# Strided attention of batch 3 in two visits of quarter-array matmuls instead of six of full-array ones, with a second buffer for the transposed strided keys

## The chip, the core and the metric

The kernel runs on one core of a Trainium2 chip. A core has a matmul engine (PE, here called by its matmuls; PEld are its weight loads, which overlap them), a vector engine (DVE), a scalar engine (ACT), a general engine (POOL) and a queue engine (SP). Each works through its own list of instructions in order, and they wait for one another by semaphores. PE writes only to PSUM, eight banks of 2 KiB per partition; DVE and ACT read it from there. Transfers between the memory outside of the core and SBUF are issued here by POOL (with a cast from f32 to bf16) and by SP (transposes and outputs), and run on 16 DMA engines.

The metric is the time of one execution on the device in microseconds, lower is better. Times of single instructions come from a profiled execution.

## The reference

Attention with two kinds of heads, then a two-layer network with a squared ReLU:

```python
B, H, S, D = 8, 8, 576, 64; stride = 32
scores = q @ k.T / sqrt(D)
mask_local = (rel >= 0) & (rel < stride)                  # heads 0 to 3, rel = row - column
mask_strided = (rel >= 0) & (column % stride == row % stride)   # heads 4 to 7
attn = softmax(where(mask, scores, -1e9))
x = (attn @ v).transpose(0, 2, 1, 3).reshape(4608, 512)
out = (relu(x @ w_in) ** 2) @ w_out                       # 512 -> 2048 -> 512
```

In a strided head a token attends to the earlier tokens of its own residue modulo 32, 18 at most. So such a head splits into 32 separate problems of 18 by 18.

## The kernel before

**Main loop.** After batch 0, which has a list of its own, the program is one list of 288 groups of matmuls: nine chunks c of 512 tokens, each with 16 groups of the first layer (`mm1`, L863) and 16 of the second (`mm2`, L969). A group is four matmuls of 512 columns, except in the last two chunks. Chunk 2 is groups 64 to 95 and chunk 3 groups 96 to 127; chunk 3 (tokens 1536 to 2047) is the first that reads attention of batch 3 (tokens 1728 to 2303). A first-layer group goes to one of two PSUM banks (4 and 5), from which ACT takes the ReLU (L869) and DVE the square (L873). A second-layer bank is copied by ACT to `y` (L973), every fourth group, and sent out on SP's queue (L977).

**Attention between the groups.** The text `PLAN` names for each group the attention steps that are put into the program ahead of it. A step issues its matmuls there, and may put off what follows on ACT and DVE by some groups (`later`, `tick`; `put_off` does it for bank readers). The order on every engine is thus the order of this text; nothing is rearranged afterwards. Steps of the local heads are `G` (scores of a batch's two pairs, L599, then the exponentials L610 and masks L606), `D` (outputs, L822, with L827 and L828) and `E` (DMA transpose into `xt`, L837). `xt` are the four tiles of transposed attention that `mm1` reads.

**Banks of the attention steps.** After group 32 they have six banks (6, 7, 0, 1, 3 and 2) in a list, and each use moves a bank to the list's end. `bank("pt")` takes the first; `bank_two` takes the pair of neighbours that was used longest ago. `step_G` takes all six, in order, and fills them two at a time:

```python
bk = [bank("pt") for _ in range(6)]
bk = [bk[0::2], bk[1::2]]
...
nc.tensor.matmul(bk[row][t // 4][:, c:c + QL], ...)
```

**Strided heads, two ways.** The four strided heads of a batch are packed so that three heads of one residue make a block of 54 by 54 (the fourth head's residues are packed by three). `OLD` names the batches that use the first way.

- *Full array* (batches 1 and 3): two residues of odd and even parity lie on the diagonal of one 128 by 128 weight tile whose rest is zero. Keys are copied into `kbd` (`step_K`, L382 and L386, one visit for each parity), values into `vbd` (`spread_v_str`, L447). Scores take three visits (`s3.0`, `s3.1`, `s3.2`: `step_SS`, L623, exponential L624, mask L626), outputs three (`x3.0` to `x3.2`: `step_XX`, sums L634, outputs L637, logarithm L640, exponential L642, products L650 and L657).
- *Quarter array* (batches 2, 4, 5, 6, 7): matmuls with 64 by 64 weights, four at a time on the four quarters. Scores take one visit (`s4`: `step_S4`, L687 straight from the transposed keys, L692 from the copy `kcs` of the fourth head), in four banks; outputs one visit (`x4+2+5`: `step_X4`, sums L751, outputs L756), in three pairs of banks for parts 0, 1 and 2. ACT takes logarithm and exponential of the sums of a part (L722, L723), DVE multiplies (six L735 for part 0, six for part 1, four L728 for part 2). The two numbers say by how many groups the work of parts 1 and 2 on ACT and DVE is put off.

**Loading.** POOL loads strided keys and queries in rows (`k_t`, `q_t`, L365), SP transposes them by DMA into `kT_s` and `qT_s` (L370; steps `Xnk`, `Xnq`). There are two buffers for `qT_s` and one for `kT_s`. Values come by POOL: two loads into `v_st` for the first way (L440, L443), four into `v_s` for the second (L432, L436).

In the plan, batch 3 stands like this: keys copied ahead of groups 68 and 69, scores at 72, 73 and 76, outputs at 75, 88 and 90. `G4`, the score step of batch 4's local heads, stands ahead of group 94.

Of the kernel before, what the change touches and what calls it, by code (L numbers as in the profile page):

```python
# [67 lines left out]
56: C4k C4q  # L68
57: V3 R12kv
58: V4 R12qa  # L70
60: B30v
61: B31v R13qv
62: R13ka
63: U4
64: X4q
66: Y17
67: Y16 C5q
68: k30v
69: k31v
70: X4k  # L80
71: C5k Q20k Q21q Q20q
72: Q21k s3.0
73: s3.1
75: x3.0
76: s3.2
80: G3
81: H3v
84: D12.0 D13.0
85: D12.1 D13.1
86: E12  # L90
87: E13
88: x3.1
90: x3.2
93: H4v
94: G4
96: k41v
# [53 lines left out]
def kernel(  # L150
# [24 lines left out]
    NP2 = STRIDE // 2  # L175
    NG = 5
    NH = NG + 1
    OLD = (1, 3)
    NB = NP2 + NH
    NS = NP2 // 2  # L180
    W3 = 3 * NA
# [9 lines left out]
    rows = ctx.enter_context(ExitStack())  # L191
# [7 lines left out]
    v_st = rows.enter_context(tc.tile_pool(name="v_st", bufs=1, side="right"))  # L199

    PS = bass.MemoryType.PSUM
    strTs = {nm: rows.enter_context(tc.tile_pool(name=f"strT{nm}", bufs=n, side="right")) for nm, n in (("q", 2), ("k", 1))}
    psum = ctx.enter_context(tc.tile_pool(name="psum", bufs=1, space=PS))
    psb = psum.tile([128, 8, 512], FP32, name="psb")
    all_banks = [psb[:, i] for i in range(8)]
# [171 lines left out]
    def step_K(b, par, copy):  # L377
        o = str_T[b, "k"]
        r = slice(64 * par, 64 * par + 64) if b in OLD else slice(0, 128)
        kb = kbd[r, :, 64 * par:64 * par + W3]  # L380
        if b in OLD:
            copy(kb[:, 0:NP2], o[r, 0:NP2, 0:W3])  # L382
        to = kb[:, NP2:NB] if b in OLD else kcs[b % 2][:, :, 0:W3]
        src = o[r, :, W3:SP_]
# [42 lines left out]
    def load_v_str(b):  # L427
        if b not in OLD:
            t = vs_pool.tile([128, (2 * NS + NH) * D], BF16, name="v_s")
            w, wh = 2 * NS * D, NH * D  # L430
            for f in range(2):
                nc.gpsimd.dma_start(out=t[64 * f:64 * f + W3, 0:w],  # L432
                                    in_=v[b, 4:7].rearrange("h (m r) d -> (h m) (r d)", r=STRIDE)[:, w * f:w * (f + 1)])
                src = v[b, 7]
                src = bass.AP(src.tensor, src.offset + wh * f, [[2 * NG * D, 3], [RW, NA], [1, wh]])
                nc.gpsimd.dma_start(out=t[64 * f:64 * f + W3, w:w + wh], in_=src)  # L436
            v_str[b] = t
            return
        t = v_st.tile([W3, 2 * NB * D], BF16, name="v_st")
        nc.gpsimd.dma_start(out=t[:, 0:RW], in_=v[b, 4:7].rearrange("h (m r) d -> (h m) (r d)", r=STRIDE))  # L440
        src = v[b, 7]
        src = bass.AP(src.tensor, src.offset, [[2 * NG * D, 3], [RW, NA], [1, 2 * (NG + 1) * D]])
        nc.gpsimd.dma_start(out=t[:, RW:2 * NB * D], in_=src)  # L443
        v_str[b] = t
# [727 lines left out]
    for line in PLAN.strip().splitlines():  # L1172
        n, words = line.split(":")
# [42 lines left out]
```

## Time and profile before

| what | us |
|---|---|
| median of 3 runs (lowest to highest) | 296.67 (295.76 to 296.91) |
| the profiled execution | 296.19 |
| its span, first to last instruction | 294.5 |
| PE busy | 285.5 |
| DVE busy | 206.3 |
| ACT busy | 169.4 |
| POOL busy | 85.5 |

The two kinds of matmuls of the main loop, L863 with 130.8 us and L969 with 99.2 us, hold most of PE's time. Their mean duration of 379 ns is longer than their distance, since one begins while the one before it drains; where a row gives a length, the distance to the start of the next row is what a piece of work costs.

How to read a row of the timeline: start and length in us, engine, line, operation, output and inputs, tile or shape, count, and in brackets how long the engine stood still before it and what ended that. A row with a count is several equal instructions put together. A few matmul records can be missing, so a count may be one short. In the list of waits the columns are who waited, for whom, total, times and longest.

### The profile page before, as it was taken

What the parts mean: (1) busy time and instruction counts of PE and PEld (TensorE: products, weight loads), DVE (VectorE), ACT (ScalarE), POOL (GpSimd) and SP (SyncE); (2) the same over time, 40 slices, a digit from 0 to 9 for tenths busy, and PEclk for the clock granted to TensorE, in tenths of its full rate; (3) what the DMA queues carried; (4) which work ended last, traced back from release to release, by engine and by line L of the source; (5) the groups of instructions that cost most, each with busy time, mean ns of one, the idle gap of its engine ahead of it and who ended that gap; (6) DMA issues with size and microseconds to landing.
All of it is one profiled execution on the core that took longest, in us unless ns stands there. A gap on an engine that the chain in (4) does not pass through costs nothing.

```text
span 294.5 us, 6425 instructions
## 1 busy us (share of the span) xinstructions
PE 285.5 (97%) x2441; PEld 153.6 (52%) x2477; DVE 206.3 (70%) x531; ACT 169.4 (58%) x320; POOL 85.5 (29%) x133
## 2 busy tenths in 40 slices
PE   7899999999999999999999999999999999999994
PEld 3554555544445454454445444454444444984594
DVE  5667797685577755667367836683389979958983
ACT  3767846774758736674567446654675566206610
POOL 8884443073025036146400940000000014103300
PEclk9999999999999999999999999999999999999999
DMA  7999999999999999989997997521011210030003
GB/s 144 187 210 208 198 202 183 212 212 101 135 249 140 153 168 173 184 107 138 216 158 132 136 217 138 108 58 73 36 20 48 82 38 1 0 115 30 1 2 142
DMA packets 91086, 37.23 MB, mean 126 GB/s; under 512 B 77392, under 2 KB 83896, under 8 KB 91056
## 3 DMA queue, kind: packets, MB, share of 16 engines
q0 software_dynamic: 49968, 18.14, 58.9%
q1 hardware_dynamic: 40944, 18.62, 31.6%
q8 instruction: 19, 0.31, 0.4%
q14 instruction: 11, 0.09, 0.1%
q10 hardware_dynamic: 144, 0.07, 0.1%
HBM read 36.83 MB, written 9.44 MB: 157 GB/s over the span
## 4 chain that ended last, share of the span: by engine, by line
PE 93%; DMA 3%; issue 1%; POOL 1%; DVE 0%; DVEq 0%; POOLq 0%
PE psb L863 42%; PE psb L969 33%; PE psb L939 9%; DMA vl<-in_v_dram 3%; PE psb L822 2%; PE psb L599 1%; PE psb L502 1%; PE psb L554 1%; PE psb L751 1%; PE psb L687 1%; PE psb L756 1%; POOL xt L306 0%; PE psb L637 0%; PE psb L844 0%; PE psb L623 0%
## 5 line engine op out<-in xcount | busy, mean ns | idle before, releaser
L863 PE MATMUL psb<-xt,w_in 128*128 128x512 bf16 x557 | 130.8, 379 | 0.9
L869 ACT ACTIVATE r<-psb 128x512 bf16<-128x512 f32 x144 | 85.6, 599 | 46.2 <-PE psb L863 43.0
L969 PE MATMUL psb<-w_out_b,g_sb 128*128 128x512 bf16 x432 | 99.2, 379 | 1.4 <-issue 0.8
L863 PEld LDWEIGHTS <-w_in 128*128 128x128 bf16 x576 | 53.7, 98 | 60.0 <-issue 1.1
L873 DVE TENSOR_TENSOR g_sb<-r 128x512 bf16<-128x512 bf16 x112 | 46.8, 422 | 39.9 <-ACT r L869 38.7
L969 PEld LDWEIGHTS <-g_sb 128*128 128x128 bf16 x448 | 41.8, 98 | 47.5
L973 ACT COPY y<-psb 128x512 f32<-128x512 f32 x28 | 16.6, 591 | 38.9 <-PE psb L969 38.8
L908 POOL CAST sa<-g_sb 128x256 fp32r<-128x256 bf16 x16 | 9.6, 603 | 96.6 <-DVE g_sb L903 96.6
L735 DVE TENSOR_TENSOR xt<-psb,rv 64x144 bf16<-64x144 f32 x60 | 18.7, 311 | 9.2 <-ACT rv L723 8.4
L828 DVE TENSOR_TENSOR x_l<-psb,rinv 96x384 bf16<-96x384 f32 x28 | 15.5, 553 | 1.0
L606 DVE TENSOR_TENSOR e<-e,mask_all 128x576 bf16<-128x576 bf16 x20 | 8.4, 458 | 10.5 <-ACT e L610 10.3
L903 DVE TENSOR_TENSOR g_sb<-r 128x512 bf16<-128x512 bf16 x32 | 13.0, 420 | 2.9 <-ACT r L869 2.9
L610 ACT ACTIVATE e<-psb 128x384 bf16<-128x384 f32 x30 | 12.0, 513 | 4.2 <-PE psb L599 4.2
L365 POOL DMA_DIRECT2D q_t<-in_q_dram x6 | 3.2, 536 | 38.1 <-DMA qT_s<-q_t 22.4
L294 POOL DMA_DIRECT2D k_l<-in_k_dram x16 | 11.7, 736 | 4.1 <-DMA k_t<-in_k_dram 1.6
L294 POOL DMA_DIRECT2D q_l<-in_q_dram x16 | 11.6, 732 | 3.4 <-DMA k_t<-in_k_dram 2.0
L939 PE MATMUL psb<-t,s 128*128 128x256 f32 x96 | 12.2, 283 | 0.0
L365 POOL DMA_DIRECT2D k_t<-in_k_dram x6 | 3.3, 553 | 30.2 <-DMA kT_s<-k_t 28.2
L939 PEld LDWEIGHTS psb<-t,s 128*128 128x128 f32 x96 | 11.6, 188 | 0.0
L951 DVE TENSOR_TENSOR y<-psb,y 128x256 f32<-128x256 f32 x19 | 8.1, 424 | 4.3 <-PE psb L939 3.5
L453 POOL DMA_DIRECT2D vl<-in_v_dram x8 | 9.8, 1227 | 3.7 <-PE psb L969 2.8
L650 DVE TENSOR_TENSOR xt<-psb,rv 64x144 bf16<-64x144 f32 x24 | 7.5, 311 | 4.5 <-ACT rv L642 4.2
(153 smaller groups left out, 321.8 us busy)
## 6 DMA issues: line engine op xcount, KB each, us to landing
out_dram<-y SPq DMA_DIRECT2D x35, 256.0 KB, 2.8
vl<-in_v_dram POOLq DMA_DIRECT2D x8, 288.0 KB, 9.1
w_out_b<-in_moe_w_out_dram POOLq DMA_DIRECT2D x4, 512.0 KB, 14.9
q_t<-in_q_dram POOLq DMA_DIRECT2D x7, 288.0 KB, 6.6
k_t<-in_k_dram POOLq DMA_DIRECT2D x7, 288.0 KB, 6.3
w_in<-in_moe_w_in_dram POOLq DMA_DIRECT2D x2, 768.0 KB, 13.5
k_l<-in_k_dram POOLq DMA_DIRECT2D x16, 72.0 KB, 8.1
q_l<-in_q_dram POOLq DMA_DIRECT2D x16, 72.0 KB, 7.2
```

The source lines that it names most:

```text
L294: nc.gpsimd.dma_start(out=t[:, :, hh, :], in_=src[b, 2 * p + hh].rearrange("(t p) d -> p t d", p=QL))
L453: nc.gpsimd.dma_start(out=t[32:128, :, :, :, 0:D].rearrange("p u h t d -> p (u h t) d"), in_=v[b, 0:4].rearrange("h (t p) d -> p (h t) d", ...
L610: nc.scalar.activation(e[:, row, 4 * QL * i:4 * QL * (i + 1)], bk[row][i][:, 0:4 * QL], AF.Exp, scale=scale)
L735: nc.vector.tensor_tensor(to[:, :, :, n * part:n * (part + 1), par], both[half(par), :, 0:w].rearrange("c f (a h m) -> c h m f a", a=n, h= ...
L828: nc.vector.tensor_tensor(x, po[0:QL, :, 0:D], rinv[0:QL].to_broadcast([QL, NL, D]), op=ALU.mult)
L863: nc.tensor.matmul(ph, w_in_tile(kk, ff), xt[kk][:, 512 * c:512 * (c + 1)], start=(kk == order[0]), stop=(kk == order[-1]))
L869: nc.scalar.activation(r, ph, AF.Relu)
L873: later(1, lambda: nc.vector.tensor_tensor(g[:, ff, :], r, r, op=ALU.mult))
L903: nc.vector.tensor_tensor(g[:, ff, :], r, r, op=ALU.mult)
L939: nc.tensor.matmul(pa, a, b, start=k == 0 and n not in "273", stop=k == 7, skip_group_check=True)
L969: nc.tensor.matmul(py, g[:, ff, 128 * j:128 * (j + 1)], w_out_b[:, ff, :], start=(ff == 0), stop=(ff == 15))
L973: nc.scalar.copy(y, py)
```

## The change

`3` is taken out of `OLD`, so that batch 3 goes the second way; the plan's steps for it become one score visit at group 72 and one output visit at group 88, with the work of part 1 put off by one group and that of part 2 by three. Its values are loaded by four transfers into `v_s`, at the same place in the list. The copies into `vbd` (`B30v`, `B31v`) and one of two key copies (`k30v`) go; `k31v` now copies the fourth head's keys into `kcs`. Transposed strided keys get a second buffer, so that a key transpose of any later batch does not wait for the score visit of the batch before it (`step_S4` reads them directly, and with one buffer batch 4's transpose, ahead of group 70, would stand ahead of batch 3's score visit at 72).

```diff
-60: B30v
-61: B31v R13qv
+61: R13qv
...
-68: k30v
 69: k31v
 70: X4k
 71: C5k Q20k Q21q Q20q
-72: Q21k s3.0
-73: s3.1
-75: x3.0
-76: s3.2
+72: Q21k s3
 80: G3
 81: H3v
-84: D12.0 D13.0
+83: D12.0 D13.0
 85: D12.1 D13.1
 86: E12
 87: E13
-88: x3.1
-90: x3.2
+88: x3+1+3
 93: H4v
 94: G4
...
-    OLD = (1, 3)
+    OLD = (1,)
...
-    strTs = {nm: rows.enter_context(tc.tile_pool(name=f"strT{nm}", bufs=n, side="right")) for nm, n in (("q", 2), ("k", 1))}
+    strTs = {nm: rows.enter_context(tc.tile_pool(name=f"strT{nm}", bufs=n, side="right")) for nm, n in (("q", 2), ("k", 2))}
```

The outputs `D12.0` and `D13.0` of the local heads move one group forward. On PE the six visits (44 score matmuls, 6 of sums and 44 of outputs in batches 1 and 3 together, so 22, 3 and 22 here) are replaced by 44 score matmuls, 12 of sums and 44 of outputs on quarters of the array. SP's list keeps the same instructions in the same order; POOL's has two loads more.

## The prediction

> **What bounds the kernel now.** I read the page first (engines, slices, chain), then the waits of the matmul engine, then its timeline around the two places that change.
>
> ```profile
> span 294.5 us, 6425 instructions
> PE 285.5 (97%) x2441; PEld 153.6 (52%) x2477; DVE 206.3 (70%) x531; ACT 169.4 (58%) x320; POOL 85.5 (29%) x133
> PEclk9999999999999999999999999999999999999999
> PE 93%; DMA 3%; issue 1%; POOL 1%; DVE 0%; DVEq 0%; POOLq 0%
> ```
>
> PE is busy 97% of the span and is 93% of the chain that ended last. DVE at 70% and ACT at 58% hang on it. The clock row has a 9 in all 40 slices.
>
> ```profile
> PE psb L986 <- DVE xt L1101: 1.3, 1, 1.3
> PE psb L969 <- issue: 0.8, 5, 0.2
> PE psb L554 <- DVE kTl L509: 0.4, 1, 0.4
> ```
>
> These are the three longest waits of PE (total, times, longest). The first and third belong to batch 0. Behind them PE waits for no engine and no transfer, only five times for "issue", never over 0.2 us. So a change in the middle counts in full if it takes matmul time away from PE or makes PE wait, and counts nothing if it only relieves DVE, ACT or a queue.
>
> **The change, part by part.** First the matmuls themselves. This is PE's timeline from the first scores of batch 3 to the score step of the local heads of batch 4 (G4). The columns are start, length, line, names, shape and count. Lengths overlap since matmuls are pipelined, so I price a visit from its start to the start of what follows it.
>
> ```profile
> 90.37 0.36 PE L623 MATMUL psb<-qT_s,kb 128*128 128x54 bf16 x8
> 90.58 1.02 PE L863 MATMUL psb<-xt,w_in 128*128 128x512 bf16 x4
> 91.44 0.37 PE L623 MATMUL psb<-qT_s,kb 128*128 128x54 bf16 x8
> 91.64 1.89 PE L863 MATMUL psb<-xt,w_in 128*128 128x512 bf16 x8
> 93.37 0.35 PE L634 MATMUL psb<-e,ones_bd 128*128 128x432 bf16 x1
> ...
> 93.77 1.02 PE L863 MATMUL psb<-xt,w_in 128*128 128x512 bf16 x3
> 94.63 0.31 PE L623 MATMUL psb<-qT_s,kb 128*128 128x54 bf16 x6
> 94.78 3.69 PE L863 MATMUL psb<-xt,w_in 128*128 128x512 bf16 x16
> 98.40 0.69 PE L599 MATMUL psb<-qT,kTl 64*128 64x96 bf16 x24
> 99.02 3.63 PE L969 MATMUL psb<-w_out_b,g_sb 128*128 128x512 bf16 x15
> ...
> 106.67 0.35 PE L634 MATMUL psb<-e,ones_bd 128*128 128x432 bf16 x1
> ...
> 107.07 1.89 PE L969 MATMUL psb<-w_out_b,g_sb 128*128 128x512 bf16 x8
> 108.79 0.30 PE L634 MATMUL psb<-e,ones_bd 128*128 128x324 bf16 x1
> ...
> 109.09 3.61 PE L969 MATMUL psb<-w_out_b,g_sb 128*128 128x512 bf16 x16
> 112.64 0.68 PE L599 MATMUL psb<-qT,kTl 64*128 64x96 bf16 x24
> ```
>
> Removed scores: 0.21 (90.37 to 90.58) + 0.20 (91.44 to 91.64) + 0.15 (94.63 to 94.78) = 0.56 us. Removed outputs: 0.40 (93.37 to 93.77) + 0.40 (106.67 to 107.07) + 0.30 (108.79 to 109.09) = 1.10 us. What replaces them already runs for the other batches:
>
> ```profile
> 74.10 0.29 PE L751 MATMUL psb<-e,ones 54*64 54x216 bf16 x4
> ...
> 124.26 0.44 PE L687 MATMUL psb<-qT_s,kT_s 64*64 64x54 bf16 x32
> ...
> 124.73 1.04 PE L863 MATMUL psb<-xt,w_in 128*128 128x512 bf16 x3
> ...
> 160.87 0.29 PE L751 MATMUL psb<-e,ones 54*64 54x216 bf16 x4
> ...
> 161.59 8.81 PE L969 MATMUL psb<-w_out_b,g_sb 128*128 128x512 bf16 x39
> 170.33 0.68 PE L599 MATMUL psb<-qT,kTl 64*128 64x96 bf16 x24
> ```
>
> A scores visit takes 0.47 us (124.26 to 124.73, 44 matmuls), an outputs visit 0.72 us (160.87 to 161.59, 56 matmuls). PE gains 1.66 - 1.19 = 0.47 us. That is all that there is to gain: the removed work is 1.66 us in all, 0.56% of the span.
>
> [...]
>
> Second, when the outputs are read. The new visit writes all six attention banks in 0.72 us, and they come free one pair after another, as DVE multiplies each part by its reciprocal sums: twelve L735 products for parts 0 and 1, four L728 products for part 2. Then comes G4, six groups later, and it takes six banks itself, the longest unused first. So its matmuls 1 to 8 go to the pair of part 0, 9 to 16 to that of part 1, and 17 to 24 to that of part 2. In the built program number 17 waits for the second L728 product and number 18 for the fourth. Before the change these two banks were those of the third outputs visit. This is ACT's and DVE's work on such visits:
>
> ```profile
> 107.92 0.56 ACT L642 ACTIVATE rv<-rv 128x432 f32<-128x432 f32 x1
> ...
> 108.51 1.93 DVE L650 TENSOR_TENSOR xt<-psb,rv 64x144 bf16<-64x144 f32 x6 [2.80 <-ACT rv L642]
> 110.48 1.42 DVE L657 TENSOR_TENSOR xt<-psb,rv 64x270 bf16<-64x270 f32 x4
> ...
> 162.62 3.90 DVE L735 TENSOR_TENSOR xt<-psb,rv 64x144 bf16<-64x144 f32 x12 [0.59 <-ACT rv L723]
> 166.72 1.96 DVE L728 TENSOR_TENSOR xt<-psb,rv 64x162 bf16<-64x162 f32 x4 [0.20 <-ACT rv L723]
> ...
> 81.09 1.97 DVE L728 TENSOR_TENSOR xt<-psb,rv 64x162 bf16<-64x162 f32 x4
> ```
>
> Before, the last bank was free at 110.48 + 1.42 = 111.90, ahead of G4's start at 112.64. After:
>
> - The visit starts at 106.67 - 0.56 + 0.47 - 0.40 = 106.18.
> - Its first product comes 1.84 later, as at this place before (106.67 to 108.51; a copy of y on ACT goes ahead of the logarithm there, and will again): 108.02.
> - Twelve products take 3.90: 111.92. Four take 1.96: 113.88.
> - G4 would start at 112.64 - 0.47 = 112.17 and take 0.62 (98.40 to 99.02), so it would be done at 112.79. Its 18th matmul waits until 113.88, a hand-over costs 0.03 (107.92 + 0.56 to 108.51 on ACT and DVE), and seven of 24 matmuls remain, 0.18: 114.09.
>
> The stall is 1.30 us, and net of the gain the path is 1.30 - 0.47 = 0.83 us longer. A check from batch 5: there the last product ends at 168.68 and the 17th matmul of its G step falls due at 170.33 + 0.41 = 170.74, 2.06 us of slack at ten groups' distance. A group is 0.86 us (90.58 to 91.44), so at six groups 3.44 of distance are gone and 1.38 us are missing; 0.20 of that is the gap ahead of L728 there.
>
> Bounds of the stall: the shortest chain would be batch 5's without that gap, 168.68 - 160.87 - 0.20 = 7.61 from the visit's start against my 7.70, so 1.2 us; the longest is batch 2's, 74.10 to 81.09 + 1.97, 8.96, so 2.6 us. I take 1.30, since the work on ACT at this place is that of the row at 107.92 and not batch 2's. Queued behind the waiting matmul are the rest of PE's program, two groups of outputs and then the next chunk; nothing after it has slack that would give time back, as the waits show.
>
> Third, the local outputs `D12.0` and `D13.0` of batch 3, one group earlier. They need the masked exponentials of the first row, two of four masks:
>
> ```profile
> 100.11 1.78 DVE L606 TENSOR_TENSOR e<-e,mask_all 128x576 bf16<-128x576 bf16 x4
> ...
> 102.48 0.53 PE L822 MATMUL psb<-vl,e 128*128 128x65 bf16 x12
> ```
>
> PE will come to them at 102.48 - 0.49 (what is gone by then) - 0.86 = 101.13, the two masks, which move with G3, end at 100.11 + 0.89 - 0.49 = 100.51. So 0.6 us of slack hide the move, and it costs at most what the masks lose of it.
>
> Fourth, what costs nothing. The spread values and two sets of key copies leave DVE, and the logarithms leave the first-layer stage of ACT; PE waited for neither there, so matmuls hide them. If that cover were gone, a delay on ACT would hold one of two banks of the first layer. The queues:
>
> ```profile
> 60.76 0.51 POOL L440 DMA_DIRECT2D v_st<-in_v_dram x1
> 61.26 0.64 POOL L443 DMA_DIRECT2D v_st<-in_v_dram x1
> ...
> 96.10 1.79 SPq L396 DMA_TRANSPOSE qT<-q_l x1
> ...
> 124.78 2.53 SPq L370 DMA_TRANSPOSE kT_s<-k_t x1
> ```
>
> Values of batch 3 come by four issues instead of two, some 1.15 us more on POOL's queue (0.51 + 0.64). The row and column loads of batch 4 stand behind them, and their first transpose runs only at 96.10. The second key buffer frees the key transpose of batch 5, which ran at 124.78, right behind the score visit (124.26 to 124.73) that read the one buffer. It gains SP at most some tenths here, and PE waits for no transfer. If a load did come late, G4 would be its first reader. Both parts are 0, from -0.1 to +0.3.
>
> Sum: 296.19 (the profiled execution, span 294.5) + 0.83 = 297.0. That execution is 0.48 below the median of the runs, 296.67; from the median it is 297.5. I say 297.2.
>
> **The rivals.**
>
> - *No stall.* G4 finds its banks free, since the products run shorter or it takes them in another order. Then only the 0.47 is left: 295.7, or 296.2 from the median. For it: batches 4 to 7 run the same two visits without a wait. Against it: they have nine groups or more between outputs and G, here it is six, and the row at 166.72 gives no shorter product. Chance 0.13.
> - *Slower by more than the measurement can tell.* The chain of logarithms and products runs as in batch 2, 8.96 us, because ACT puts other copies between its parts. Then the 18th matmul waits until 106.18 + 8.96 = 115.14, the stall is 2.56 and the path 2.1 longer: 298.3, or 298.8 from the median. The change is over 0.5% (1.48 us) slower from the point where the last L728 product ends after 114.5. Against it: batch 2's extra copies (L414) stand in no group from 88 to 93. Chance 0.14.
> - *The clock gives way at the stall.* If the clock were halved for as long as the 16 matmuls from 109.09 to 112.64 take, 3.55 us more: 300.6. The row of the clock speaks against it, and so does the wait of 1.3 us at the start, which left that row at 9. [...] Chance 0.04.
>
> **How the numbers follow.** The forecast, a stall of 1.2 to 1.9 us, has 0.66; 0.03 is for what I don't see. The range goes from the no-stall case on its own time (295.7) to batch 2's chain from the median (298.8). Within 0.5%, about what a measurement of this kernel can tell from no change, lie the forecast but for its upper end and nearly all of the no-stall case: 0.71. Slower are the second and third rival and that upper end with a poor draw of runs: 0.24. Faster by 1.48 us asks for nearly all of the removed 1.66 us as gain: 0.05.
>
> **What would show it.** In the profile after: scores and outputs of batch 3 in 0.47 and 0.72 us; PE waiting once over 1 us inside G4 for the L728 products, with the last of them ending near 113.9; G4's end near 114.1; no other new wait. The prediction is wrong if G4's 24 matmuls run through in 0.62 us, if that wait is over 2 us, if PE waits for a transfer, or if the clock row shows less than 9 there.

## The result, and the profile after

The kernel after takes 297.8 us (median of 9 runs), the kernel before 296.26 us beside it (9 runs). The ratio is 1.0047, with a 95% interval of 1.0034 to 1.0061: slower by about half a per cent. Medians here and below are of all runs, while ratios leave out the runs that are more than 1.5% above the fastest of their kernel (one of nine here on each side, seven of twelve in `before_pe106` below). The profiled execution of the kernel after took 298.75 us, 0.95 above the median, with a span of 297.0.

In the file after, a line has a number that is 6 less than in the file before (G4's matmul, L599, is now L593; the products L735 and L728 are L729 and L722; the copy to `y` L973 is L967). This is the timeline of TensorE around the two visits of batch 3 and G4, in the profile after; the columns are start, length, engine, line, names, shape and count, and in brackets an idle time with what ended it:

```profile
90.78 0.44 PE L681 MATMUL psb<-qT_s,kT_s 64*64 64x54 bf16 x32
...
91.25 7.11 PE L857 MATMUL psb<-xt,w_in 128*128 128x512 bf16 x32
...
106.65 0.29 PE L745 MATMUL psb<-e,ones 54*64 54x216 bf16 x4
...
107.37 5.35 PE L963 MATMUL psb<-w_out_b,g_sb 128*128 128x512 bf16 x24
112.66 0.51 PE L593 MATMUL psb<-qT,kTl 64*128 64x96 bf16 x16
113.34 0.21 PE L593 MATMUL psb<-qT,kTl 64*128 64x96 bf16 x1 [0.17 <-DVE xt L722]
114.33 0.33 PE L593 MATMUL psb<-qT,kTl 64*128 64x96 bf16 x7 [0.77 <-DVE xt L722]
114.59 1.90 PE L963 MATMUL psb<-w_out_b,g_sb 128*128 128x512 bf16 x8
```

The scores visit takes 91.25 - 90.78 = 0.47 us, the outputs visit 107.37 - 106.65 = 0.72. G4 now comes in three pieces: 16 matmuls run, the 17th waits for a product, the 18th waits for a later one, and the last seven run through. From its first matmul to what follows it G4 takes 114.59 - 112.66 = 1.93 us in place of 0.62, so the stall is 1.31. The idle times in the brackets (0.17 and 0.77) are smaller than that, since the ends of matmuls are modelled; the starts are not. The same in the timeline of VectorE:

```profile
108.40 3.89 DVE L729 TENSOR_TENSOR xt<-psb,rv 64x144 bf16<-64x144 f32 x12 [2.95 <-ACT rv L717]
112.32 1.96 DVE L722 TENSOR_TENSOR xt<-psb,rv 64x162 bf16<-64x162 f32 x4
```

The last of the four L722 products ends at 112.32 + 1.96 = 114.28, and the 18th matmul of G4 starts at 114.33. The list of TensorE's waits (total, times, longest) has two new lines behind batch 0. One is this stall. The other is a single wait of 0.60 us for the weights of the first layer, at 21.5 us and so long before the steps that change; in `after_again`, the same kernel once more, it is not there. The clock row of the page stays at 9:

```profile
PE psb L593 <- DVE xt L722: 0.9, 2, 0.8
...
PE psb L857 <- DMA w_in<-in_moe_w_in_dram: 0.6, 1, 0.6
...
PEclk9999999999999999999999999999999999999999
```

What does all that cost the path? Two marks stand on both sides of the change in both kernels: the outputs of batch 2 and the scores of batch 4. Before, they start at 74.10 and at 124.26 (rows in the prediction). TensorE's timeline after:

```profile
74.41 0.29 PE L745 MATMUL psb<-e,ones 54*64 54x216 bf16 x4
...
125.42 0.44 PE L681 MATMUL psb<-qT_s,kT_s 64*64 64x54 bf16 x32
```

From mark to mark it is 50.16 us before and 51.01 after: 0.85 more. The spans differ by 297.0 - 294.5 = 2.5. Of the other 1.65, the start of the kernel (up to the first mark) has 0.31, and it varies as much from one profile to the next. The rest, 1.34, is lost in the last fifteen microseconds, in which no step of the plan was changed. Here is that end before, with TensorE, VectorE and the issues of output DMAs on SP's queue:

```profile
280.80 4.03 PE L939 MATMUL psb<-t,s 128*128 128x256 f32 x32
...
282.08 0.42 DVE L951 TENSOR_TENSOR y<-psb,y 128x256 f32<-128x256 f32 x1 [0.34 <-issue]
...
288.16 2.26 SPq L954 DMA_DIRECT2D out_dram<-y  x3
...
288.45 2.05 PE L939 MATMUL psb<-tb,s 128*128 128x256 f32 x16
...
290.51 0.39 SPq L946 DMA_DIRECT2D out_dram<-y  x1
```

And after:

```profile
281.97 4.34 PE L933 MATMUL psb<-t,s 128*128 128x256 f32 x32
...
283.61 0.42 DVE L945 TENSOR_TENSOR y<-psb,y 128x256 f32<-128x256 f32 x1 [0.69 <-issue]
...
289.64 3.23 SPq L948 DMA_DIRECT2D out_dram<-y  x3
...
289.93 2.05 PE L933 MATMUL psb<-tb,s 128*128 128x256 f32 x16
...
292.96 0.38 SPq L940 DMA_DIRECT2D out_dram<-y  x1
```

Two things are different. The block of 32 `t,s` matmuls takes 4.34 in place of 4.03, because the first sum into `y` on VectorE comes 0.35 us later, after 0.69 of "issue" (nothing that the profile shows) in place of 0.34. And three output DMAs that took 2.26 us from the first one's start to the third one's end now take 3.23, so that the next one goes out at 292.96 and not at about 292.0. From the start of the last 16 matmuls to the end of the span it is 294.5 - 288.45 = 6.05 before and 297.0 - 289.93 = 7.07 after.

### The profile page after: what moved, and what is told of

The parts are those of the page before. It is cut to its first block, busy times and chain, and to the rows that moved or that the text cites. A ratio compares the mean times of both kernels' runs of the same rounds, so it can differ in the third digit from the quotient of the medians.

```text
span 297.0 us, 6567 instructions
## 1 busy us (share of the span) xinstructions
PE 288.3 (97%) x2530; PEld 152.9 (51%) x2530; DVE 204.7 (69%) x526; ACT 169.8 (57%) x320; POOL 86.5 (29%) x135
## 4 chain that ended last, share of the span: by engine, by line
PE 90%; DMA 4%; POOL 2%; DVE 1%; issue 1%; DVEq 0%; POOLq 0%
PE psb L857 41%; PE psb L963 32%; PE psb L933 9%; DMA w_in<-in_moe_w_in_dram 4%; PE psb L816 2%; PE psb L593 1%; PE psb L745 1%; PE psb L681 1%; PE psb L496 1%; PE psb L750 1%; DVE xt L722 1%; PE psb L548 1%; POOL w_in L459 0%; DVE xt L729 0%; POOL xt L300 0%
## 5 line engine op out<-in xcount | busy, mean ns | idle before, releaser
L963 PE MATMUL psb<-w_out_b,g_sb 128*128 128x512 bf16 x448 | 101.1, 379 | 0.0
L967 ACT COPY y<-psb 128x512 f32<-128x512 f32 x28 | 16.5, 589 | 39.0 <-PE psb L963 38.9
L729 DVE TENSOR_TENSOR xt<-psb,rv 64x144 bf16<-64x144 f32 x72 | 22.4, 312 | 12.3 <-ACT rv L717 11.3
L722 DVE TENSOR_TENSOR xt<-psb,rv 64x162 bf16<-64x162 f32 x24 | 11.2, 468 | 1.1 <-ACT rv L717 0.5
```

The lines of the kernel that those rows point to most:

```text
L722: nc.vector.tensor_tensor(t, both[half(par), f, 0:w].rearrange("c (a g m) -> c g m a", a=n, g=3), rv[half(par), w * f:w * (f + 1)].rearran ...
L729: nc.vector.tensor_tensor(to[:, :, :, n * part:n * (part + 1), par], both[half(par), :, 0:w].rearrange("c f (a h m) -> c h m f a", a=n, h= ...
L963: nc.tensor.matmul(py, g[:, ff, 128 * j:128 * (j + 1)], w_out_b[:, ff, :], start=(ff == 0), stop=(ff == 15))
L967: nc.scalar.copy(y, py)
```

## The experiments

The theories, as the expectations number them: (1) the loss is the stall of G4 on the products, less the 0.47 that the shorter visits gain; (2) a second loss of half a microsecond or more elsewhere, by the second key buffer or at the start or the end; (3) the quarter-array matmuls themselves cost more than their rows say. After the first runs two came in for the end of the kernel: (4) the place where blocks of instructions are fetched has moved, and (5) something that the change leaves behind.

The table gathers what the profiles of all kernels show, each worked out as above, with the span to a tenth: from batch 2's outputs to batch 4's scores, the last block of 32 `t,s` matmuls, and from the last 16 matmuls to the end of the span.

```
kernel                mark to mark   t,s block   last 16 to end   time, ratio (95% interval)
before                   50.16         4.03          6.05         1
after                    51.01         4.34          7.07         297.80  1.0047 (1.0034 to 1.0061)
after_again              51.02         4.33          7.24         298.51  1.0080 (1.0064 to 1.0097)
keys2_alone              50.07         4.03          6.02         296.27  1.0005 (0.9992 to 1.0018)
outputs_86               49.78         4.34          7.04         297.07  1.0024 (1.0001 to 1.0048)
outputs_89               53.43         4.36          6.55         300.21  1.0136 (1.0111 to 1.0160)
after_dve5               51.03         4.03          7.17         297.66  1.0042 (1.0024 to 1.0060)
after_pe150              51.02         4.35          5.67         300.35  1.0101 (1.0054 to 1.0148)
before_pe106             50.08         4.03          6.90         303.42  1.0090 (1.0045 to 1.0135)
after_both58             51.03         4.03          5.61         296.62  1.0016 (0.9998 to 1.0033)
outputs_86_both          50.03         4.03          5.61         296.04  0.9985 (0.9965 to 1.0006)
outputs_86_both58        49.79         4.03          5.65         295.40  0.9973 (0.9942 to 1.0004)
outputs_86_once_more     49.79         4.03          5.62         295.44  0.9974 (0.9953 to 0.9995)
full_all_88              53.08         4.03          5.99         299.15, one run
```

### The change again, and the second key buffer alone

The first is the kernel after, unchanged. The second is the kernel before with one edit:

```
-    ... for nm, n in (("q", 2), ("k", 1))}
+    ... for nm, n in (("q", 2), ("k", 2))}
```

> The changed kernel once more, for a second profile and a closer ratio. Theory 1 (the whole loss is the wait of G4 for the four L722 products of part 2, less the 0.47 us that the quarter-array matmuls save): PE waits again some 1.2 to 1.4 us over two matmuls of G4, and from the outputs visit of batch 2 to the scores visit of batch 4 the two profiles differ by 0.85 us; the ratio then is near 1.003, and what the first profile showed beyond that (0.3 us ahead of batch 2's visit, 1.3 us behind the last chunk's t,s matmuls) differs from profile to profile. Theory 2 (something else in the change, at the start or the end, costs another half us each time): the same 0.3 and 1.3 us come back, and the ratio stays near 1.005.

> The kernel before with the second key buffer alone; no other edit. Theory 1: no PE wait changes, ratio 1.000 within its interval. Theory 2: the buffer moves other tiles in SBUF and lets SP run ahead in its queue, and brings the part of the loss that the wait in G4 does not cover, about 0.5 us, ratio 1.002.

The repeat has the same 51.02 between the marks and the same long end, and a ratio above the first one's (1.0064 to 1.0097 against 1.0034 to 1.0061; the two intervals just do not meet, and what sets the two series apart was not followed up). The second key buffer alone is not to be told from the kernel before. So it costs nothing, and it is not what makes the end longer (6.02, 4.03). Theory 2's guess at the buffer falls; its half microsecond elsewhere is real.

### The outputs two groups earlier, and one group later

Both are the kernel after with the outputs visit of batch 3 at another group, the first with the steps ahead of it moved up too:

```
-85: D12.1 D13.1          +84: D12.1 D13.1        |  -88: x3+1+3
-86: E12                  +85: E12                |  +89: x3+1+3
-87: E13                  +86: E13 x3+1+3         |
-88: x3+1+3
```

> The changed kernel with the outputs visit of batch 3 ahead of group 86 instead of 88, so eight groups ahead of G4 instead of six; D12.1 and D13.1 go from 85 to 84, E12 to 85, E13 to 86. Theory 1: two groups are 1.72 us, more than the stall, so G4 runs through in 0.62 us; against the changed kernel 1.3 us are won, against the kernel before 0.47 us, ratio 0.998 to 0.999. Theory 2: only the wait in G4 goes, half a us is left: ratio 1.000. Theory 3 (the quarter-array matmuls or the switch of the array's shape cost more than the rows of the other batches say): the wait goes, but the way from the outputs visit of batch 2 to the scores visit of batch 4 is no shorter than before, 50.2 us.

> The changed kernel with the outputs visit one group later, ahead of 89. Theory 1: the chain of products starts a group (0.86 us) later and G4 does not, so the wait grows by that: about 2.0 us in G4 (less if ACT's copy of y no longer stands ahead of the first logarithm), and the path from batch 2's outputs to batch 4's scores is 0.6 to 0.9 us longer than in the changed kernel; ratio to the kernel before 1.005 to 1.008. Theories 2 and 3: the place of the visit does not matter, 1.005 as measured.

With the outputs at group 86, G4 runs through, and the marks are nearer to each other than before. TensorE's timeline of `outputs_86` (its lines are one less than those of the kernel after):

```profile
73.97 0.29 PE L744 MATMUL psb<-e,ones 54*64 54x216 bf16 x4
...
112.22 0.68 PE L592 MATMUL psb<-qT,kTl 64*128 64x96 bf16 x24
...
123.75 0.44 PE L680 MATMUL psb<-qT_s,kT_s 64*64 64x54 bf16 x32
```

123.75 - 73.97 = 49.78, that is 0.38 less than before, against the 0.47 that the visits gain by themselves. The quarter-array matmuls are not dearer than their rows, and theory 3 falls. Yet this kernel is still slower than the kernel before, by a little (1.0024, where 0.998 to 0.999 was expected), since the end is as long as in the kernel after: 4.34 and 7.04.

With the outputs one group later the stall grows to 2.06 us (G4 takes 114.61 - 111.93 = 2.68), near the 2.0 that was expected, and then something else comes on top: the ratio is 1.0136, where 1.005 to 1.008 was expected. TensorE after the stall in `outputs_89`, and then one row of the kernel after:

```profile
114.61 3.10 PE L963 MATMUL psb<-w_out_b,g_sb 128*128 128x512 bf16 x8
117.50 3.29 PE L857 MATMUL psb<-xt,w_in 128*128 128x512 bf16 x12
120.62 0.53 PE L816 MATMUL psb<-vl,e 128*128 128x65 bf16 x12
```

```profile
118.92 0.53 PE L816 MATMUL psb<-vl,e 128*128 128x65 bf16 x12
```

From the start of the eight matmuls behind G4 to the L816 that follows the next twelve it is 120.62 - 114.61 = 6.01 us here and 118.92 - 114.59 = 4.33 in the kernel after: 1.68 more. This is the view by windows of one microsecond: the window, its length, busy time of TensorE (with instructions), its weight loads, VectorE, ScalarE and GpSimd, then the granted clock, the DMA share and GB/s:

```profile
112.00:113.00 1.00, 0.62 (x17) 0.33 (x16) 0.94 (x3) 0.69 (x2) 1.00 (x3) 1.00 0.88 129
113.00:114.00 1.00, 0.21 (x1) 0.10 (x2) 0.94 (x3) 0.24 (x1) 1.00 (x2) 1.00 1.09 128
114.00:115.00 1.00, 0.65 (x9) 0.39 (x9) 0.94 (x3) 0.31 (x1) 1.00 (x2) 1.00 1.61 295
115.00:116.00 1.00, 1.00 (x4) 0.40 (x3) 0.85 (x4) 1.00 (x4) 0.68 (x2) 0.58 2.28 153
116.00:117.00 1.00, 1.00 (x3) 0.30 (x2) 0.82 (x2) 0.33 (x1) 1.00 (x3) 0.50 2.36 150
...
118.00:119.00 1.00, 1.00 (x5) 0.42 (x4) 0.00 (x0) 0.33 (x1) 0.46 (x1) 0.71 1.45 154
```

The granted clock falls to 0.50 some half a microsecond after the stall and stays there for about three microseconds (0.58, 0.50, 0.50 and 0.71 in the four windows from 115, 1.00 again from 119). That is where the 1.68 us go; with the 0.75 by which the stall grew they make up the 2.42 between the marks (53.43 against 51.01). It is the prediction's clock rival, a clock that gives way at the stall, at a place one group further on and at half of its price of 3.55. The same view of the kernel after:

```profile
112.00:113.00 1.00, 1.00 (x20) 0.46 (x18) 0.94 (x3) 0.00 (x0) 0.63 (x2) 1.00 2.15 188
113.00:114.00 1.00, 0.38 (x10) 0.12 (x4) 0.94 (x3) 0.87 (x2) 0.91 (x2) 1.00 2.40 152
114.00:115.00 1.00, 0.67 (x9) 0.39 (x9) 0.94 (x3) 0.33 (x1) 0.88 (x2) 1.00 1.80 266
```

There TensorE is busy 1.00, 0.38 and 0.67 of the three microseconds from 112 and the clock holds; here it is busy 0.62, 0.21 and 0.65, and the clock gives way. That is 49% busy over three microseconds here and 68% there. The busy share alone does not tell the two cases apart: in `full_all_88` below TensorE is busy for 1.06 of the 3.13 us from 83.66 to 86.79, or 34%, and the mean granted clock of that execution is 0.998, where three microseconds at 0.50 would leave 0.995 and `outputs_89` has 0.991. What makes the clock give way, no run shows.

### Where instructions are fetched

The page of every kernel lists queues of the kind "instruction", and a window of the queue view shows when a packet of them begins. TensorE's program has 53 matmuls with their weight loads more after the change (100 in place of 47 in the visits of batch 3), VectorE's five instructions less. From the pages, before and then after (queue, kind, packets, MB, share):

```profile
q8 instruction: 19, 0.31, 0.4%
```

```profile
PE 288.3 (97%) x2530; PEld 152.9 (51%) x2530; DVE 204.7 (69%) x526; ACT 169.8 (57%) x320; POOL 86.5 (29%) x135
...
q8 instruction: 20, 0.33, 0.5%
```

The weight loads (PEld) are 2530 against 2477 in the row that the prediction shows, VectorE's instructions 526 against 531. In q8 there is one packet more; 0.31 MB in 19 packets are 16 KB each. The last q8 packet begins at 279.9 before, and the last two at 272.6 and 290.8 after. The 18.2 us between those two hold 132 matmuls and 131 weight loads of TensorE; the expectations below go by 256 instructions in 18 us. The queue view of the kernel after for the tenth of a microsecond from 290.80:

```profile
q1 hardware_dynamic: 21, 0.04, 110.2%
q8 instruction: 1, 0.02, 106.2%
```

The last figure is the time that the packet took, as a share of 16 engines in the window: 1.062 x 16 x 0.1 = 1.70 us. So it lies from 290.8 to 292.5, beside the packets of the outputs, and the slow third issue of the output DMAs begins at 291.6. Four kernels test whether the place of these packets makes the end longer. They put small matmuls in the place of six of the nine idle ones at the start, or repeat a small memset of VectorE there:

```
after_dve5:       -    nc.vector.memset(kTl[0][:, 0:32], 0.0)
                  +    [nc.vector.memset(kTl[0][:, 0:32], 0.0) for _ in range(6)]
before_pe106:     -    warm(9)
                  +    pw = bank("py")
                  +    [nc.tensor.matmul(pw, idle[:, 0:128], idle, ...) for _ in range(3)]
                  +    [nc.tensor.matmul(pw[0:32, 0:32], idle[:, 0:32], idle[:, 0:32], ...) for _ in range(59)]
after_pe150:      the same with range(81)
outputs_86_both:  outputs_86 with both, range(81)
```

> The kernel before with 53 more TensorE matmuls: six of the nine idle matmuls of the start are replaced by 59 small ones (32 columns), so that TensorE's program has as many instructions (4916) as that of the kernel after; attention, outputs and the expert layer are untouched. Theory 4 (the last 12 us of the kernel after lose 1.0 us because a block of TensorE's instructions, queue q8, is fetched at 290.8, 1.1 us before the end of its matmuls, where the kernel before has its last fetch at 279.9): the fetch appears here too, some 7 us ahead of where the kernel before has it and once more near the end; the third output DMA of L954 in the tail takes about 1300 ns to issue in place of 333, from the last 16-matmul block's start to the end of the span takes 7.05 in place of 6.05, and the time is 297.2 (ratio 1.0034), if the start of the expert layer does not move. Rival 5 (the tail is longer because of what the change itself leaves behind: key buffer, order of VectorE's work, fewer DMA sections): 6.05 and 296.3. The block of 32 t,s matmuls ahead of it keeps 4.03 by both.

> The kernel after with five more VectorE instructions: the small memset of L1099 at the start six times, so that VectorE's program is again as long as before (612). Theory 4: the 0.35 us that the first L945 of the last chunk came late (0.69 with nothing waited for, at 283.61, where a fetch in q14 begins at 283.2) was a fetch of VectorE's own instructions; it falls elsewhere now, the t,s block of 32 takes 4.03 in place of 4.34, and the time is 0.3 less than that of the kernel after: 297.5 to 298.2 by which of its two medians one takes (ratio about 1.0055). The slow third output DMA stays at about 1300 ns. Rival 5: 4.34 as in the kernel after, and no gain.

> The kernel after with 75 more matmuls: six of the nine idle ones of the start are replaced by 81 small ones, so that TensorE's program is 256 instructions longer than that of the kernel before, which puts its fetches (one 18 us after the other, 290.8 less 272.4) where the kernel before has them. Theory 4: the fetch at 290.8 is gone, the third output DMA takes 332 ns again, last block's start to end 6.05 in place of 7.05, and the time is 1.0 less than the kernel after's: 296.9 to 297.4 (ratio about 1.003). The t,s block stays at 4.34. Rival 5: 7.05 and 298.

> The kernel with the strided outputs at group 86 (outputs_86), with both paddings: 75 more small matmuls and five more VectorE memsets at the start. Theory 4: t,s block 4.03 and last block to end 6.05, that is 1.3 less than outputs_86, and from batch 2's outputs to batch 4's scores 49.8 against 50.16 before: 295.8 to 295.9, ratio 0.9987, faster than both kernels by a little. Rival 5: as outputs_86, 297.1, ratio 1.0024.

Five memsets at the start take the 0.31 us away 280 us later. `after_dve5`, TensorE and VectorE:

```profile
281.68 4.03 PE L933 MATMUL psb<-t,s 128*128 128x256 f32 x32
...
282.96 0.42 DVE L945 TENSOR_TENSOR y<-psb,y 128x256 f32<-128x256 f32 x1 [0.34 <-issue]
```

The matmuls do the same for the output DMAs, in both directions. The kernel before, whose attention is untouched, gets a slow issue (`before_pe106`; it falls on L946, the fourth, since here the packet in q8 begins at 297.0):

```profile
295.40 2.06 PE L939 MATMUL psb<-tb,s 128*128 128x256 f32 x16
...
297.46 0.86 SPq L946 DMA_DIRECT2D out_dram<-y  x1
```

And the kernel after loses its slow issue, while the late sum on VectorE stays (`after_pe150`):

```profile
287.71 0.42 DVE L945 TENSOR_TENSOR y<-psb,y 128x256 f32<-128x256 f32 x1 [0.70 <-issue]
...
293.73 2.26 SPq L948 DMA_DIRECT2D out_dram<-y  x3
```

So each of the two losses follows the count of one engine's instructions, which is what theory 4 says and 5 does not. For TensorE the traces of all 14 kernels agree. In the six in which a q8 packet begins 0.7 to 1.6 us after the start of the last 16 matmuls, one output issue takes 0.57 to 1.39 us; in the other eight the last q8 packet begins 3.3 us or more ahead of them, and none of the last issues takes over 0.40. What the runs do not show is the link: that the packet and the outputs meet in one DMA engine is argued from their times.

For VectorE only the count is shown: the sum is late in the five kernels with 526 of its instructions and in none of the nine with 531. That a fetch holds it up is not shown. The fetches of VectorE are not told from those of other engines in q14, and in `after_dve5`, where the sum is in time, a q14 packet begins at 282.93, 0.03 ahead of it.

The times of two of the three kernels with three idle matmuls did not come out as expected (303.42 for 297.2, and 300.35 for 296.9 to 297.4). The expectation had taken the start for untouched. It wasn't. The clock row of `after_pe150` has a 5 and an 8 in its third and fourth slices (the mean over its span is 0.983), and the outputs of batch 2 begin at 78.49 in place of 74.10. In `before_pe106` they begin at 81.13; its clock row is at 9 there, but six matmuls of L502 take 0.66 us at 13.43 where, in the kernel before, they take 0.43 at 11.61. These two are read at their ends alone. The third, `outputs_86_both`, came near (296.04 for 295.8 to 295.9); of the 0.25 between the marks that it has above `outputs_86`, TensorE waits 0.18 for a transpose into `xt`.

### The change without its fetches, and the version that beats both

The paddings again, with seven of the nine idle matmuls kept and 31 small ones, on the kernel after and on `outputs_86`; the last run is the same kernel once more:

```
-    warm(9)
+    pw = bank("py")
+    [nc.tensor.matmul(pw, idle[:, 0:128], idle, ...) for _ in range(7)]
+    [nc.tensor.matmul(pw[0:32, 0:32], idle[:, 0:32], idle[:, 0:32], ...) for _ in range(31)]
```

> The kernel after with both paddings, the TensorE one now with seven of the nine idle matmuls of the start left in place of three, so that TensorE's clock comes up as before: 31 small matmuls and five small VectorE memsets, the computation untouched. Theory 4: TensorE's last fetch moves 58 instructions ahead, some 4 us (18 us for 256), to 286 or 287 and so ahead of the output DMAs of the tail; t,s block 4.03, last block to end 5.6 to 6.05. What is left of the change is then its own 0.85 from batch 2's outputs to batch 4's scores: 296.1 to 296.3 and 0.85, 297.0 to 297.1, ratio 1.003. If the prediction's mechanism were only half of the loss for another reason, the time stays at 297.7.

> The same paddings with the strided outputs at group 86. Theory 1 and theory 4 together: no stall in G4, visits 0.47 shorter, tail as before: 49.8 from batch 2's outputs to batch 4's scores, 295.7 to 295.9, ratio 0.9985 (0.998 to 0.999), and without the executions of lower clock that three idle matmuls brought. Rival 5: 297.1.

> The kernel outputs_86_both58 again on another chip or at another time, since its interval (0.9942 to 1.0004) just holds 1. If its gain is its own (visits 0.47 shorter, the end of the span some 0.4 nearer to the last matmuls than in the kernel before), the ratio is 0.9975 again, between 0.997 and 0.9985, and the interval ends below 1. If the median of the first time was luck, it comes out at 0.9985 to 1.0.

The last fetch in q8 now begins at 286.1 in `after_both58`, where no output is issued, and both losses are gone:

```profile
282.24 4.03 PE L933 MATMUL psb<-t,s 128*128 128x256 f32 x32
...
289.60 2.26 SPq L948 DMA_DIRECT2D out_dram<-y  x3
289.89 2.06 PE L933 MATMUL psb<-tb,s 128*128 128x256 f32 x16
```

Its last 16 matmuls are 295.5 - 289.89 = 5.61 from the end, 0.44 less than before. That 0.44 belongs to the change and not to the paddings. The instructions in the traces place it behind all outputs, in the closing of GpSimd's program: from its first signal to the other engines to the end of the span it is 1.10 us in all four kernels without the change (before, `keys2_alone`, `full_all_88`, `before_pe106`) and 0.66 in all ten with it, the kernel after among them. GpSimd has two loads more in those ten (135 instructions for 133); why its closing is shorter with them is open. The slow issue thus costs the kernel after 7.07 - 5.61 = 1.46, of which the closing gives 0.44 back. With the 0.85 of the stall, 0.41 more than before was to be expected, and it is 296.62 - 296.08 = 0.54 (1.0016, an interval that holds 1). `outputs_86_both58` has no stall and is 0.7 to 0.9 us faster than the kernel before, in two sessions: 295.40 against 296.08 and 295.44 against 296.30. The first interval just holds 1, the second (0.9953 to 0.9995) does not. Of that, 0.37 is the shorter visits (49.79 for 50.16), and 0.4 the shorter closing.

### Full-array visits, all at group 88

```
-75: x3.0
-84: D12.0 D13.0          +83: D12.0 D13.0
-88: x3.1
-90: x3.2                 +88: x3.0 x3.1 x3.2
```

> The kernel before with batch 3's three full-array output visits all at group 88 (D12.0 and D13.0 one group earlier, as in the kernel after). Theory 1 (VectorE's products of all six banks cannot be through before G4): G4 waits for the product line here too, but less, 0.2 to 0.6, since the three visits take 1.10 in place of 0.72 and the first banks are free to be read 0.4 earlier. Theory 3 (the quarter-array form itself makes the wait): G4 runs through in 0.68 as before.

G4 waits here too. TensorE, VectorE's last products, and a wait of TensorE's further ahead:

```profile
115.24 0.55 PE L597 MATMUL psb<-qT,kTl 64*128 64x96 bf16 x17
116.11 0.33 PE L597 MATMUL psb<-qT,kTl 64*128 64x96 bf16 x7 [0.32 <-DVE xt L655]
116.37 1.90 PE L967 MATMUL psb<-w_out_b,g_sb 128*128 128x512 bf16 x8
```

```profile
114.66 1.40 DVE L655 TENSOR_TENSOR xt<-psb,rv 64x270 bf16<-64x270 f32 x4
```

```profile
85.27 1.06 PE L861 MATMUL psb<-xt,w_in 128*128 128x512 bf16 x3 [1.61 <-ACT y L971]
```

From start to start G4 takes 1.13 in place of 0.62: 0.51, within the 0.2 to 0.6. So it is six banks at one place so near to G4 that make the stall, in either form of matmul. In the kernel after it is 0.80 longer for two reasons. G4 comes 0.36 sooner after the start of the visit (6.01 us, against 115.24 - 108.87 = 6.37 here), and the last product ends 0.44 later (7.63 after that start, against 116.06 - 108.87 = 7.19), mainly since the last four products take 1.96 in place of 1.40. The time of this run is no measure of the stall: a transpose took 7.32 us on SP's queue (2.77 at this place before), the next ones came late, ScalarE waited 4.34 for one of them with a copy that frees a bank behind it, and TensorE 1.61 for that copy. Whether the edit has a part in that was not tried.

## Why the prediction was right, and what it missed

The time, 297.8, is within the range and 0.6 above the 297.2. That is nearer than the sum itself came: beside the kernel before, at 296.26, the loss is 1.54 where the sum had 0.83, and the forecast stood on a median of 296.67, from three runs, and a profiled execution. To that extent the nearness is luck. The steps of the prediction, in their order:

*The exchange of visits.* Worked out were 0.47 and 0.72; measured are 0.47 and 0.72. The rows give 25 ns for each of the 22 full-array score matmuls (0.56 us in all) and 11 ns for each of the 44 on quarters (0.47 us). `outputs_86` shows the gain where nothing takes it back, 0.38 of the 0.47; the other 0.09 was not followed up.

*The stall.* This step carries the forecast, and it held in its place, its cause and its size. The 17th matmul of G4 waits for one product and the 18th for the last; the stall is 1.31 against 1.30, and the loss between the marks 0.85 against 0.83. The single times are off by tenths that cancel out: with the 0.31 of the later start taken off, the visit starts 0.16 later than worked out (106.65 - 0.31 = 106.34 for 106.18), and the last product ends 7.63 after it, not 7.70. That the losses between the marks agree so well is luck too. Where the first-layer matmuls behind G4 begin, the kernel after is 1.03 further from the first mark (116.33 - 74.41 = 41.92, against 114.99 - 74.10 = 40.89); 0.18 of it comes back in these twelve matmuls, 2.59 from start to start in place of 2.77, for which no wait is listed. The first rival (no stall) and the second (batch 2's longer chain, a stall of 2.56) did not come about.

*The local outputs one group earlier, the queues, the second buffer.* All were put at 0. No line in TensorE's waits after the change names them, and the buffer alone is at 1.0005. The prediction had also named a wait of TensorE for a transfer as a sign of being wrong; the one that there is, for the weights of the first layer at 21.5, is no step of the change and does not come again in `after_again`.

*The clock.* It held, as forecast. But it held narrowly: with the visit one group later it fell to 0.50. The halved clock of this rival was an assumption of the author's when its 4% were given: the trace of before has a 9 in all 40 slices of its clock row. `outputs_89` shows it, at 1.68 us in place of the 3.55; that the clock falls one group further on, the trace of before could not show.

*The step that failed* is a sentence, "nothing after it has slack that would give time back": what lies behind the stall was taken for a plain shift of the old trace. Besides the 0.18 that came back, the last fifteen microseconds were not shifted alone. With a program that is 106 instructions longer on TensorE, a fetch fell beside the last outputs, at 1.46 us in the profile; with one that is five shorter on VectorE, a sum came late, at 0.31, by a fetch or otherwise; and GpSimd's closing became 0.44 shorter. These 1.3 us in all were in no term of the sum and in no rival. The range took them in only since its upper end stood for a longer stall. The median shows less of them than the profile: `after_both58`, without them, is 296.62, and the kernel after 297.80.

## What to carry to other kernels

Count banks, not only matmul time: when several visits are put together at one place, what fills their banks in 0.7 us takes VectorE 5.9 us to free. The next step that wants those banks must be further away than the whole chain, here 7.63 us from the start of the visit to the end of the last product. Here two groups earlier turned a loss of 0.85 between the marks into a gain of 0.38. And when an edit changes the number of instructions on an engine, compare the end of the kernel with the old one before you look for a reason in the edit: here a few idle instructions at the start moved a fetch away from the last transfers.

## What was not expected of the hardware

The count of an engine's instructions alone cost time at a far place here. Five fewer on VectorE put 0.35 us before one sum, with nothing that the trace names as its cause but "issue". A packet of 16 KB in q8, whose place moves with TensorE's count, 1.70 us long and beside the last outputs, goes with an output issue of 1300 ns in place of 332 and an end that is 1.46 us later than in the same kernel with that packet elsewhere (7.07 against 5.61 in `after_both58`). The packets of q8 are of 16 KB (0.31 MB in 19, before), those of q14 half as large (0.10 MB in 12, after). Behind batch 0, TensorE's waits in the kernel after name none of the 20 packets of q8: the longest are the 0.8 for the products and the 0.6 for the first layer's weights.

The granted clock fell to 0.50 in `outputs_89` after a stretch in which TensorE was busy for 49% of three microseconds, and held at 1.00 in the kernel after behind one with 68%. It was back at 1.00 after some three microseconds, at a cost of 1.68 us.
